# Weights converted without a clamp, their scale bounded by sums on TensorE, and a new table of homes for early work

## The chip, the cores and the metric

One core of one Trainium2 chip runs the whole program in one launch. The metric is the device time of one execution in microseconds (us); 514.47 us is the median of three runs of the kernel before (514.44 to 514.57).

Five engines work from instruction queues of their own: TensorE (PE; the loading of its stationary operand is listed apart as PEld), VectorE (DVE), ScalarE (ACT), GpSimd (POOL) and SyncE (SP, which here issues all DMAs).

## The reference

Windowed attention (8 batches, 8 heads, 576 positions, head size 64; a query sees itself and the 63 keys ahead of it), then a feed-forward block over all 4608 tokens (512 to 1024 to 512):

```python
scores = scale * np.matmul(q, k.transpose(0, 1, 3, 2))
scores = np.where((rel >= 0) & (rel < 64), scores, -1e9)
attn = softmax(scores); x = np.matmul(attn, v)        # tokens x 512
h = x @ w_in
solu = h * softmax(h)
ln = (solu - mean(solu)) / np.sqrt(var(solu) + 1e-6) * g_ln
return ln @ w_out
```

`w_in` and `w_out` come as 64-bit floats, all else as 32-bit ones.

## The kernel before

Tokens are worked through in 36 tiles of 128 (two windows of 64). For each tile: `scores` (TensorE, L547, into the bank pS), `softmax` (DVE, ACT; L599/L600 scale each head's row by its sum), the transposed probabilities PT (for tiles 0 to 7 `transposes` on TensorE, L654, and a copy, L659; later ones by two DMAs, L628 and L631), `values` (L680, bank pX), `moe_in` (bank pH, L707 for the first three tiles and L719 after), `moe_norm` (L734 largest value, L740 exponential, L743 product with h, which reads pH last, L751 squares, L758 power on POOL, L764 normalisation), `planes` and `turn` (halves of 16 bits, L792 and L795, and a transposing DMA) and `moe_out` (bank pO, L848 for the first tile and L858 after). pH, pS, pX and pO have one buffer each, so a tile's products there wait until the last reader of the tile before is through.

The weights are converted on the chip. `weight_block` does it for eight blocks of 1 MB (0 to 3 are w_in, 4 to 7 w_out). A block is loaded into raw (four buffers) as pairs of 32-bit words, low word first. ACT takes the absolute value of the high words, scaled by a power of two (L367, into w); POOL or DVE brings the top three bits of the low words to the bottom (L370 or L371); DVE clamps the result and keeps each partition's largest value (L374, `accum_out`), shifts it left by three and joins the low bits (L377), and sets the sign (L379). w then holds the weights as 32-bit floats with their exponent shifted.

The first tiles are multiplied with w directly, in 32 bits (`moe_in` for tiles 0 to 2, `moe_out` for tile 0). Later tiles use two 16-bit planes of each weight, high and low, made by `split`: L481/L482 (high) and L484 (low, always DVE). They need a common scale, which `spread` makes from the largest values of four blocks: a reduction (L390), two operations of one column (L392, L395), a diagonal matrix and a product with ones to spread the largest over all partitions (L398, L400), a reduction (L402) and two bit operations. `in_scale` does this for w_in while tile 1 is planned, `out_scale` for w_out in the turn of tile 3 behind `moe_out` of tile 0.

The order of instructions is a written-out list. Each operation is entered in `Plan` with engine, a duration in ns, and what it reads and writes. `order` computes when each is due, counted back from TensorE's own sequence, and then places them one by one, the most urgent that is ready first, with a latency of 150 ns between engines. Operations of TensorE that are marked loose may leave its sequence. Where TensorE would have nothing to do ahead of the first output (`shown`), `order` inserts fillers: 128x128 products of the identity into pO (L971), one for each 235 ns of 0.7 of the gap.

`HOMES` gives the engine for flexible operations, by task, tile and half; where it has no entry, a default holds (`home`): scale DVE for tiles 0 and 1 and else POOL; PT ACT, from tile 4 on DVE for the second half; join POOL up to tile 7 and then ACT; norm POOL; high planes ACT; planes POOL for tiles 1 and 2 and else DVE; high ACT; low bits POOL.

Of the kernel before, what the change touches and what calls it, by code (L numbers as in the profile page):

```python
# [11 lines left out]
BF16 = mybir.dt.bfloat16  # L12
# [20 lines left out]
W_SCALE = 2.0 ** 8  # L33
# [19 lines left out]
    ("scale", 0, 1): "POOL", ("scale", 1, 0): "POOL", ("scale", 1, 1): "ACT", ("scale", 3, 0): "DVE",  # L53
    ("scale", 4, 0): "ACT", ("scale", 4, 1): "DVE", ("scale", 5, 0): "ACT", ("scale", 5, 1): "ACT",
    ("scale", 6, 0): "ACT", ("scale", 6, 1): "ACT", ("scale", 8, 0): "DVE", ("scale", 8, 1): "DVE",
    ("scale", 10, 0): "ACT",
    ("PT", 0, 0): "DVE", ("PT", 1, 0): "DVE", ("PT", 1, 1): "DVE", ("PT", 2, 0): "DVE", ("PT", 4, 1): "ACT",
    ("PT", 5, 1): "ACT", ("PT", 6, 0): "DVE", ("PT", 7, 1): "ACT",
    ("join", 0, 0): "ACT", ("join", 1, 0): "ACT", ("join", 1, 1): "ACT", ("join", 3, 0): "ACT",
    ("join", 3, 1): "ACT", ("join", 4, 0): "ACT", ("join", 4, 1): "ACT",  # L60
    ("soft", 9, 0): "DVE", ("soft", 9, 1): "DVE", ("soft", 10, 0): "ACT", ("soft", 10, 1): "ACT",
    ("norm", 0, 1): "DVE", ("norm", 2, 0): "DVE", ("norm", 2, 1): "DVE", ("norm", 3, 1): "DVE",
    ("norm", 4, 0): "DVE", ("norm", 5, 1): "DVE",
    ("high planes", 2, 0): "DVE", ("high planes", 2, 1): "POOL", ("high planes", 3, 0): "POOL",
    ("high planes", 3, 1): "POOL", ("high planes", 4, 0): "POOL", ("high planes", 4, 1): "POOL",
    ("high planes", 5, 0): "POOL", ("high planes", 5, 1): "POOL", ("high planes", 6, 0): "DVE",
    ("high planes", 6, 1): "DVE",
    ("planes", 3, 0): "POOL", ("planes", 3, 1): "POOL", ("planes", 4, 0): "POOL", ("planes", 5, 0): "POOL", ("planes", 5, 1): "POOL", ("planes", 7, 0): "POOL",
    ("planes", 8, 0): "POOL",
    ("high", 1, 0): "DVE", ("high", 2, 0): "POOL", ("high", 2, 1): "POOL", ("high", 3, 0): "POOL",  # L70
    ("high", 4, 1): "POOL", ("high", 7, 0): "POOL",
    ("low bits", 4, 0): "DVE",
# [23 lines left out]
class Plan:  # L96
# [125 lines left out]
def tile_window_attention_solu_moe(  # L222
# [331 lines left out]
    def softmax(t):  # L554
# [10 lines left out]
        elif t in MASKED:  # L565
            for r in range(2):
# [4 lines left out]
                plan.op("DVE", 80, lambda hs=hs: nc.vector.tensor_scalar_mul(  # L571
# [71 lines left out]
    def transposes(t):  # L643
        if t >= SOFT_BY_DMA:
            return
        for x in range(2):
# [5 lines left out]
            def emit(x=x, pA=pA):  # L652
# [6 lines left out]
                e, 600, lambda x=x, pA=pA, e=e: copy_on(e)(PT(t)[:, 4 * x:4 * x + 4], pA()),  # L659
# [13 lines left out]
    def values(t):  # L673
# [16 lines left out]
        plan.op("ACT", 600, lambda: nc.scalar.mul(X(t, 0), PX(t), XS(t, 1)), [("pX", t), ("xs", t)], [("xH", t)])  # L690
        plan.op("DVE", 690, lambda: nc.vector.scalar_tensor_tensor(
# [32 lines left out]
    def moe_norm(t):  # L724
# [12 lines left out]
        if scaled:  # L737
            plan.op("DVE", 80, lambda: nc.vector.tensor_scalar(
# [7 lines left out]
        plan.op("DVE", 80, lambda: nc.vector.tensor_scalar_mul(nmean(), sp(), -1.0 / DFF), [key(2)], [key(4)])  # L746
        plan.op("DVE", 80, lambda: nc.vector.tensor_scalar(
# [38 lines left out]
    def planes(t):  # L786
        if not crosses(t):
            return
        for h in range(2):
# [5 lines left out]
            plan.op(e, {"POOL": 1450, "DVE": 690}[e], lambda hs=hs, e=e: units[e].tensor_sub(  # L795
# [41 lines left out]
    def moe_out(t):  # L837
# [24 lines left out]
        def ot():  # L862
# [158 lines left out]
```

## Time and profile before

| | us |
|---|---|
| median of three runs | 514.47 |
| profiled execution, its own time | 513.94 |
| its span | 512.0 |
| PE busy | 498.4 (97%) |
| DVE busy | 393.8 (77%) |
| ACT busy | 343.5 (67%) |
| POOL busy | 267.7 (52%) |
| fillers (L971), 166 of them, part of PE busy | 22.7 |

The profile is of one execution. The span runs from the first to the last instruction; the execution's own time lies 1.94 us above it. A busy time is the sum of an engine's instructions in a stretch without overlap. [...] A number in brackets behind an instruction is the idle time of its engine ahead of it, with what released it.

### The profile page before, as it was taken

Reading aid. Unit: us, or ns where it says so; the run is one execution under the profiler, and the core shown is the slowest. Engines: PE = TensorE matmul, PEld = TensorE weight load, DVE = VectorE, ACT = ScalarE, POOL = GpSimd, SP = SyncE. Lnnn points to the kernel's source line nnn. Section 1 sums busy time; section 2 is a strip of 40 time slices with the busy share of each in tenths; the row PEclk is TensorE's granted clock in tenths of the full one; section 3 lists DMA queues with packets and bytes.
Section 4 is the critical chain, followed back from the end, with each engine's and each line's share of the span. In section 5 each row is a group of like instructions: output and inputs, shape, how many; then the busy total and the mean of one; then the engine's idle time right before and its main releaser. Section 6 shows DMA issues by size and latency. Waiting matters only on the chain.

```text
span 512.0 us, 11781 instructions
## 1 busy us (share of the span) xinstructions
PE 498.4 (97%) x4297; PEld 269.3 (53%) x4297; DVE 393.8 (77%) x890; ACT 343.5 (67%) x978; POOL 267.7 (52%) x459
## 2 busy tenths in 40 slices
PE   8899989999999999999999999999999999999996
PEld 8575654455555555555555545555555555544452
DVE  4999999989778788888777777777777777765430
ACT  5378677787876677777777767777777777764240
POOL 5626515468555655555366656666666666662110
PEclk9999999999999999999999999999999999999999
DMA  8990316578999999999999999999999999769311
GB/s 348 402 359 33 90 56 156 173 190 199 283 247 268 247 268 255 258 292 259 263 258 253 262 250 249 255 270 268 267 276 227 262 272 229 186 176 235 104 41 42
DMA packets 157449, 115.59 MB, mean 226 GB/s; under 512 B 129872, under 2 KB 130128, under 8 KB 156880
## 3 DMA queue, kind: packets, MB, share of 16 engines
q1 hardware_dynamic: 157392, 114.84, 84.6%
q8 instruction: 34, 0.56, 0.4%
q14 instruction: 23, 0.19, 0.1%
HBM read 41.42 MB, written 41.42 MB: 162 GB/s over the span
## 4 chain that ended last, share of the span: by engine, by line
PE 81%; DVE 9%; DMA 3%; SPq 2%; ACT 1%; issue 1%; ACTq 0%
PE pO L858 31%; PE pH L719 30%; PE pX L680 7%; PE pS L547 6%; DMA raw<-pd 3%; PE pH L707 2%; SPq L804 1%; PE pO L848 1%; DVE w_inL L484 1%; DVE e L743 1%; PE t L654 1%; PE pX L858 1%; DVE w_outL L484 1%; DVE mst L734 1%; PE pO_filler L971 1%; DVE w L377 1%
## 5 line engine op out<-in xcount | busy, mean ns | idle before, releaser
L858 PE MATMUL pO<-w_outH,yT 128*128 128x512 f16 x544 | 167.6, 380 | 0.3 <-ACT ot L869 0.3
L719 PE MATMUL pH<-w_inH,xH 128*128 128x512 f16 x528 | 161.8, 379 | 2.4 <-DVE mst L743 2.1
L600 POOL TENSOR_SCALAR sS<-sS,rec 128x128 f32<-128x128 f32 x240 | 100.9, 439 | 101.6 <-DVE rec L596 101.0
L858 PEld LDWEIGHTS <-yT 128*128 128x128 f16 x840 | 79.6, 98 | 97.8 <-issue 6.2
L719 PEld LDWEIGHTS <-xH 128*128 128x128 f16 x792 | 75.1, 98 | 91.0 <-ACT xH L690 2.2
L584 ACT ACTIVATE sS<-sS,nmx 128x128 f32<-128x128 f32 x264 | 102.0, 390 | 18.1 <-DVE nmx L580 12.8
L858 PE MATMUL pO<-w_outL,yT 128*128 128x512 f16 x272 | 103.1, 379 | 0.7 <-DVE w_outL L484 0.7
L719 PE MATMUL pH<-w_inL,xH 128*128 128x512 f16 x264 | 99.0, 379 | 0.0
L758 POOL TENSOR_TENSOR mst<-mst,neghalf 128x1 f32<-128x1 f32 x36 | 20.3, 564 | 91.0 <-DVE mst L756 82.4
L740 ACT ACTIVATE e<-pH,mst,xscale 128x1024 f32<-128x1024 f32 x33 | 39.6, 1201 | 39.0 <-DVE rec L593 30.1
L734 DVE TENSOR_REDUCE mst<-pH 128x1 f32<-128x1024 f32 x36 | 44.0, 1223 | 26.6 <-PE pH L719 26.4
L869 ACT ACTIVATE ot<-pO,bound 128x512 f32<-128x512 f32 x34 | 23.3, 685 | 57.5 <-PE t_x L451 47.8
L764 POOL TENSOR_SCALAR e<-e,mst 128x512 f32<-128x512 f32 x66 | 52.0, 795 | 16.9 <-DVE mst L759 14.6
L620 POOL COPY raw<-sS 128x1024 uint16<-128x1024 uint16 x52 | 52.8, 1043 | 1.1 <-DVE sS L600 1.1
L795 DVE TENSOR_TENSOR pl<-e,pl 128x512 f16<-128x512 f32 x55 | 49.0, 926 | 1.7 <-ACT pl L792 1.6
L584 ACT ACTIVATION_READ_ACCUMULATOR sS<-sS,nmx 128x1 f32 x264 | 50.0, 189 | 0.0
L743 DVE CUSTOM_DVE_ANT_0 e<-pH,e 128x1024 f32<-128x1024 f32 x36 | 43.7, 1215 | 3.0 <-ACT e L740 3.0
L751 ACT ACTIVATE unread<-e,mst 128x1024 bf16<-128x1024 f32 x36 | 40.9, 1137 | 5.7 <-DVE mst L746 5.7
L754 DVE SCALAR_TENSOR_TENSOR mst<-mst 128x1 f32<-128x1 f32 x36 | 27.1, 752 | 21.8 <-ACT unread L751 21.8
L547 PE MATMUL pS<-qk 64*64 64x128 f32 x1152 | 39.8, 275 | 0.0
L575 DVE SCALAR_TENSOR_TENSOR sS<-pS,maskNone 128x1024 f32<-128x1024 f32 x26 | 31.7, 1221 | 9.9 <-PE pS L547 9.9
L514 ACT COPY vx<-v 64x512 f32<-64x512 f32 x63 | 38.9, 617 | 0.4
(129 smaller groups left out, 708.0 us busy)
## 6 DMA issues: line engine op xcount, KB each, us to landing
qk<-qk SPq DMA_DIRECT2D x36, 640.0 KB, 4.8
yd<-pl SPq DMA_DIRECT2D x33, 512.0 KB, 3.3
pd<-raw SPq DMA_DIRECT2D x28, 512.0 KB, 4.1
v<-vS SPq DMA_DIRECT2D x36, 256.0 KB, 3.6
y<-ot SPq DMA_DIRECT2D x35, 256.0 KB, 3.3
raw<-w_in SPq DMA_DIRECT2D x4, 1024.0 KB, 10.7
raw<-w_out SPq DMA_DIRECT2D x4, 1024.0 KB, 8.0
yT<-yd SPq DMA_TRANSPOSE x33, 5.1
```

Of the source, the lines that this page charges most:

```text
L547: nc.tensor.matmul(PS(t)[half * WIN:(half + 1) * WIN, r, p], q[rs, p, half * WIN:(half + 1) * WIN], keys, start=t not in MASKED, stop=t no ...
L584: plan.op("ACT", 580, lambda h=h: nc.scalar.activation(SS(t)[:, h], PS(t)[:, h // NPAIR, h % NPAIR] if t in MASKED else SS(t)[:, h], AF.Ex ...
L600: SS(t)[:, h], SS(t)[:, h], rec()[:, h:h + 1]) if e == "ACT" else units[e].tensor_scalar(
L620: plan.op(e, {"POOL": 1050, "ACT": 1000, "DVE": 700}[e], lambda x=x, e=e: copy_on(e)(PP(t)[:, :, 4 * x:4 * x + 4].rearrange("p k h n -> p ...
L719: plan.op("PE", 218, lambda n=n, c=c, k=k, w=w: nc.tensor.matmul(PH(t)[:, hs], X(t, k)[:, c], w(c, h), start=(n == 0), stop=(n == len(pass ...
L734: plan.op("DVE", 1230, lambda: nc.vector.tensor_reduce(nmax(), PH(t), axis=AX.X, op=ALU.max, negate=True), [("pH", t)], [key(0)])
L740: plan.op("ACT", 1320, lambda: nc.scalar.activation(E(t), PH(t), AF.Exp, bias=nmax(), scale=XS(t, 2) if scaled else 1.0, accum_out=se()), ...
L743: plan.op("DVE", 1310, lambda: nc.vector.tensor_tensor_reduce(E(t), PH(t), E(t), scale=1.0, scalar=0.0, op0=ALU.mult, op1=ALU.add, accum_o ...
L751: plan.op("ACT", 1330, lambda: nc.scalar.activation(unread, E(t), AF.Square, bias=nmean(), scale=1.0, accum_out=ss()), H2 + [key(4)], [key ...
L764: plan.op(e, {"POOL": 820, "DVE": 400}[e], lambda h=h, hs=hs, e=e: units[e].tensor_scalar(E(t)[:, hs], E(t)[:, hs], nmean(), kk(), ALU.add ...
L795: plan.op(e, {"POOL": 1450, "DVE": 690}[e], lambda hs=hs, e=e: units[e].tensor_sub(PL(t)[:, 1, hs], E(t)[:, hs], PL(t)[:, 0, hs]), [("e", ...
L858: plan.op("PE", 216, lambda f=f, i=i, x=x, k=k, y=y, w=w: nc.tensor.matmul(PO(), Y(t, y)[:, f], w(i, x), start=(f == k == 0), stop=(f == N ...
```

## The change

The clamp L374 goes. The first bit operation now reads w and writes its result into the low words of raw, the second joins the sign and writes w. The scale's bound is no longer the largest value but a sum: `add_up` takes the top 16 bits of each low word of raw (which then hold the absolute weight) as bf16, and multiplies 128 columns of them at a time, as the stationary operand, with one column of ones, eight products added up in one column of a PSUM tile `sums` in the bank pO. `spread` reduces four such columns. One small operation of `spread` goes. The powers of two of the scale are fitted to it. The fillers now write into `sums` too, and `shown` looks for the first tile's output alone.

```diff
-SHIFT = 2.0 ** -48
+SHIFT = 2.0 ** -112
-W_SCALE = 2.0 ** 8
+W_SCALE = 2.0 ** 13
...
-                shown = any(k[0] == "pO" for k in self.ops[i][4])
+                shown = ("pO", 0) in self.ops[i][4]
...
-        plan.op("DVE", 1210, lambda: nc.vector.tensor_scalar(
-            tf(), tf(), EXP_HI * SHIFT, EXP_LO * SHIFT, ALU.min, ALU.max, accum_out=most), [W],
-            [W, ("most", i)], lat=200)
-        plan.op("DVE", 1240, lambda: nc.vector.scalar_tensor_tensor(
-            t(), t(), 3, lo(), ALU.logical_shift_left, ALU.bitwise_or), [R, W], [W])
-        plan.op("DVE", 1240, lambda: nc.vector.scalar_tensor_tensor(
-            t(), hi(), -0x80000000, t(), ALU.bitwise_and, ALU.bitwise_or), [R, W], [W])
+        plan.op("DVE", 1270, lambda: nc.vector.scalar_tensor_tensor(
+            lo(), t(), 3, lo(), ALU.logical_shift_left, ALU.bitwise_or), [W], [R])
+        plan.op("DVE", 1380, lambda: nc.vector.scalar_tensor_tensor(
+            t(), hi(), -0x80000000, lo(), ALU.bitwise_and, ALU.bitwise_or), [R], [W])
+    def add_up(i):
+        def emit():
+            raw = T("raw", i, [P, 2, 512, 2], I32)
+            tops = raw.rearrange("p a n w -> p (a n w)").bitcast(BF16)
+            for c in range(8):
+                nc.tensor.matmul(
+                    sums()[:, P + i:P + i + 1], tops[:, 4 * c * P + 1:4 * (c + 1) * P:4], onesB[:, :1],
+                    start=(c == 0), stop=(c == 7))
+        plan.op("PE", 500, emit, [("raw", i), ("pO", "sums")], [("most", i)], loose=True)
+    def sums():
+        return T("pO", "sums", [P, DM], pool=ps_o)
...
     def spread(blocks, m, b, inv, name, gain=None):
+        for i in blocks:
+            add_up(i)
...
         small(lambda: nc.vector.tensor_reduce(
-            m, bound[:, blocks.start:blocks.stop], axis=AX.X, op=ALU.max), [("most", i) for i in blocks], [("m", name)])
-        small(lambda: nc.vector.tensor_scalar(
-            b.bitcast(I32), m.bitcast(I32), 3, 0, ALU.logical_shift_left, ALU.bitwise_or),
-            [("m", name)], [("b", name)])
+            m, sums()[:, P + blocks.start:P + blocks.stop], axis=AX.X, op=ALU.max),
+            [("most", i) for i in blocks] + [("pO", "sums")], [("m", name)], 150)
...
-                    T("pO", "filler", [P, DM], pool=ps_o)[:, :P], ident, ident, start=True, stop=True)
+                    sums()[:, :P], ident, ident, start=True, stop=True)
```

The durations in the list, in ns:

| operation | before | after |
|---|---|---|
| DVE passes of one column (`small` and others) | 80 | 145 |
| L367 on ACT; L370 on POOL | 1090; 1900 | 1150; 1330 |
| high on ACT, DVE, POOL; L484 | 600, 400, 860; 690 | 720, 490, 800; 840 |
| join on POOL, ACT, DVE | 700, 590, 400 | 880, 615, 400 |
| scale on POOL, DVE, ACT | 480, 220, 400 | 480, 340, 390 |
| PT on ACT, DVE | 600, 600 | 600, 680 |
| L690; L691; L869 | 600; 690; 580 | 680; 740; 680 |
| norm on POOL, DVE | 820, 400 | 820, 600 |
| planes on POOL, DVE | 1450, 690 | 1160, 920 |

The homes, defaults filled in, of both halves of tiles (for high and low bits: of blocks); what stays is left out, and so are tiles 7 to 12, for which the new table also has entries:

| task | before, then after |
|---|---|
| scale | 0: DVE POOL, ACT POOL; 1: POOL ACT, ACT POOL; 2: POOL POOL, ACT POOL; 3: DVE POOL, POOL POOL; 4: ACT DVE, POOL POOL; 5: ACT ACT, POOL ACT; 6: ACT ACT, POOL POOL |
| PT | 0: DVE ACT, ACT ACT; 1: DVE DVE, ACT DVE; 4: ACT ACT, DVE ACT; 6: DVE DVE, DVE ACT |
| join | 0: ACT POOL, POOL ACT; 1: ACT ACT, DVE DVE; 3: ACT ACT, DVE ACT; 4: ACT ACT, ACT POOL; 5: POOL POOL, ACT POOL |
| norm | 0: POOL DVE, POOL POOL; 2: DVE DVE, POOL POOL; 3: POOL DVE, POOL POOL; 4: DVE POOL, POOL DVE; 5: POOL DVE, POOL POOL; 6: POOL POOL, POOL DVE |
| high planes | 1: ACT ACT, ACT DVE; 2: DVE POOL, POOL POOL; 3: POOL POOL, DVE DVE; 5: POOL POOL, ACT DVE |
| planes | 3: POOL POOL, POOL DVE; 5: POOL POOL, DVE POOL; 6: DVE DVE, POOL POOL |
| high | 0: ACT ACT, POOL ACT; 1: DVE ACT, DVE POOL; 2: POOL POOL, ACT ACT; 3: POOL ACT, POOL ACT; 4: ACT POOL, DVE POOL; 5: ACT ACT, POOL POOL; 6: ACT ACT, POOL ACT |
| low bits | 1: POOL, DVE |

## Rows read from the trace of the kernel before

**Rows 1.** Busy time of each engine in three stretches (us, busy, instructions; then clock, DMA).

```profile
5.00:40.00 35.00, 32.11 (x350) 24.91 (x347) 31.58 (x65) 21.48 (x66) 13.26 (x21) 1.00 0.98 384
40.00:105.00 65.00, 60.95 (x508) 34.92 (x507) 64.10 (x153) 47.85 (x138) 30.07 (x38) 1.00 0.39 102
105.00:500.00 395.00, 393.94 (x3392) 202.77 (x3391) 297.65 (x673) 271.72 (x773) 220.20 (x380) 1.00 0.94 238
```

**Rows 2.** The same view of line L971 (fillers) alone: TensorE's products, weight loads.

```profile
5.00:40.00 35.00, 15.05 (x120) 14.06 (x120) 1.00 0.98 384
40.00:105.00 65.00, 4.30 (x32) 4.03 (x32) 1.00 0.39 102
```

**Rows 3.** Timeline of TensorE, 0 to 112 us: start, length, line, tile, count, wait.

```profile
24.96 3.96 PE L971 MATMUL pO_filler<-ident 128*128 128x128 f32 x34
...
39.33 7.11 PE L707 MATMUL pH<-w,xH 128*128 128x512 f32 x16 [0.35 <-DVE mst L743]
...
63.14 0.18 PE L451 MATMUL t_x<-vmost,some 128*128 128x2 bf16 x1
63.18 1.58 PE L971 MATMUL pO_filler<-ident 128*128 128x128 f32 x12
66.88 0.38 PE L719 MATMUL pH<-w_inH,xH 128*128 128x512 f16 x1 [2.12 <-DVE mst L743]
...
76.67 7.13 PE L848 MATMUL pO<-w,yF 128*128 128x512 f32 x16
```

**Rows 4.** Groups by line, 0 to 110 us: count, busy us, mean ns, idle before.

```profile
L379 DVE SCALAR_TENSOR_TENSOR w<-raw,w 128x1024 int32<-128x1024 int32 x8 | 11.0, 1376 | 0.0
...
L374 DVE TENSOR_SCALAR_CACHE_REDUCE w<-w 128x1024 f32<-128x1024 f32 x8 | 9.7, 1209 | 1.6 <-ACT w L367 1.6
...
L764 POOL TENSOR_SCALAR e<-e,mst 128x512 f32<-128x512 f32 x4 | 4.4, 1108 | 1.3 <-DVE mst L759 0.8 <-ACT sS L599 0.5
...
L600 DVE TENSOR_SCALAR sS<-sS,rec 128x128 f32<-128x128 f32 x12 | 3.6, 350 | 0.0
...
L764 DVE TENSOR_SCALAR e<-e,mst 128x512 f32<-128x512 f32 x4 | 2.5, 614 | 0.0
```

**Rows 5.** Busy time of line L374 alone, in two stretches.

```profile
5.00:40.00 35.00, 6.10 (x10) 1.00 0.98 384
40.00:105.00 65.00, 3.64 (x6) 1.00 0.39 102
```

**Rows 6.** Timeline of DVE, 0 to 106 us.

```profile
23.01 1.21 DVE L374 TENSOR_SCALAR_CACHE_REDUCE w<-w 128x1024 f32<-128x1024 f32 x1
...
24.15 1.21 DVE L379 SCALAR_TENSOR_TENSOR w<-raw,w 128x1024 int32<-128x1024 int32 x1
...
27.23 1.21 DVE L379 SCALAR_TENSOR_TENSOR w<-raw,w 128x1024 int32<-128x1024 int32 x1
...
44.01 0.14 DVE L746 TENSOR_SCALAR mst<-mst 128x1 f32<-128x1 f32 x1
44.07 0.14 DVE L748 TENSOR_SCALAR mst<-mst 128x1 f32<-128x1 f32 x1
...
72.73 1.21 DVE L377 SCALAR_TENSOR_TENSOR w<-w,raw 128x1024 int32<-128x1024 int32 x1
```

**Rows 7.** Timeline of ACT, 0 to 106 us.

```profile
18.51 1.17 ACT L367 ACTIVATE w<-raw 128x1024 f32<-128x1024 f32 x1 [0.93 <-DMA raw<-w_in]
...
102.60 2.44 ACT L599 ACTIVATE sS<-sS,rec 128x128 f32<-128x128 f32 x8
```

**Rows 8.** Timeline of POOL, 0 to 130 us.

```profile
20.06 1.96 POOL L370 TENSOR_SCALAR raw<-raw 128x1024 int32<-128x1024 uint32 x1
...
43.05 4.83 POOL L600 TENSOR_SCALAR sS<-sS,rec 128x128 f32<-128x128 f32 x8 [10.43 <-DVE rec L596]
...
109.80 2.80 POOL L600 TENSOR_SCALAR sS<-sS,rec 128x128 f32<-128x128 f32 x8 [0.67 <-DVE rec L596]
```

**Rows 9.** Line L451: instructions, count, shortest, median, longest in ns.

```profile
L451 PEld LDWEIGHTS <-some x33: 95/98/100, 52.6 to 467.8; 128*128 128x128 bf16 x33
```

More of the change, by code (lines that the diff above doesn't have):

```diff
@@ L52 @@
 HOMES = {
[L53 to L70, printed above, removed]
@@ L71 @@
-    ("high", 4, 1): "POOL", ("high", 7, 0): "POOL",
-    ("low bits", 4, 0): "DVE",
+    ("PT", 1, 1): "DVE", ("PT", 2, 0): "DVE", ("PT", 4, 0): "DVE", ("PT", 4, 1): "ACT", ("PT", 5, 1): "ACT",
+    ("PT", 6, 0): "DVE", ("PT", 6, 1): "ACT", ("PT", 7, 0): "DVE", ("high", 0, 0): "POOL", ("high", 1, 0): "DVE",
+    ("high", 1, 1): "POOL", ("high", 3, 0): "POOL", ("high", 4, 0): "DVE", ("high", 4, 1): "POOL",
+    ("high", 5, 0): "POOL", ("high", 5, 1): "POOL", ("high", 6, 0): "POOL", ("high", 7, 0): "POOL",
@@ new lines @@
+    ("high planes", 1, 1): "DVE", ("high planes", 2, 0): "POOL", ("high planes", 2, 1): "POOL",
+    ("high planes", 3, 0): "DVE", ("high planes", 3, 1): "DVE", ("high planes", 4, 0): "POOL",
+    ("high planes", 4, 1): "POOL", ("high planes", 5, 1): "DVE", ("high planes", 6, 0): "DVE",
+    ("high planes", 6, 1): "DVE", ("high planes", 7, 0): "POOL", ("high planes", 7, 1): "DVE",
+    ("high planes", 8, 0): "POOL", ("high planes", 8, 1): "DVE", ("high planes", 9, 1): "DVE",
+    ("high planes", 10, 0): "POOL", ("high planes", 10, 1): "POOL", ("high planes", 11, 0): "POOL",
@@ new lines @@
+    ("high planes", 11, 1): "POOL", ("join", 0, 1): "ACT", ("join", 1, 0): "DVE", ("join", 1, 1): "DVE",
+    ("join", 3, 0): "DVE", ("join", 3, 1): "ACT", ("join", 4, 0): "ACT", ("join", 5, 0): "ACT",
+    ("join", 7, 0): "ACT", ("join", 8, 0): "DVE", ("join", 10, 0): "DVE", ("join", 10, 1): "POOL",
+    ("join", 11, 1): "DVE", ("join", 12, 0): "DVE", ("join", 12, 1): "DVE", ("low bits", 1, 0): "DVE",
+    ("low bits", 4, 0): "DVE", ("norm", 4, 1): "DVE", ("norm", 6, 1): "DVE", ("norm", 7, 1): "DVE",
@@ new lines @@
+    ("norm", 8, 1): "DVE", ("norm", 9, 0): "DVE", ("norm", 10, 0): "DVE", ("norm", 10, 1): "DVE",
+    ("norm", 11, 0): "DVE", ("norm", 12, 0): "DVE", ("norm", 12, 1): "DVE", ("planes", 3, 0): "POOL",
+    ("planes", 4, 0): "POOL", ("planes", 5, 1): "POOL", ("planes", 6, 0): "POOL", ("planes", 6, 1): "POOL",
+    ("planes", 7, 1): "POOL", ("planes", 8, 0): "POOL", ("planes", 9, 0): "POOL", ("planes", 9, 1): "POOL",
+    ("planes", 10, 1): "POOL", ("planes", 11, 1): "POOL", ("planes", 12, 0): "POOL", ("planes", 12, 1): "POOL",
@@ L73 @@
+    ("scale", 0, 0): "ACT", ("scale", 0, 1): "POOL", ("scale", 1, 0): "ACT", ("scale", 1, 1): "POOL",
+    ("scale", 2, 0): "ACT", ("scale", 5, 1): "ACT", ("scale", 8, 1): "DVE", ("scale", 9, 1): "ACT",
+    ("scale", 11, 0): "ACT", ("scale", 11, 1): "ACT", ("scale", 12, 1): "DVE", ("soft", 8, 0): "DVE",
+    ("soft", 8, 1): "ACT", ("soft", 9, 1): "ACT", ("soft", 10, 0): "DVE", ("soft", 10, 1): "ACT",
+    ("soft", 11, 0): "DVE",
 }
@@ L315, in tile_window_attention_solu_moe @@
     bound = const.tile([P, NW + 12], F32, name="bound")
+    onesB = const.tile([P, 2], BF16, name="onesB")
+    nc.gpsimd.memset(onesB, 1.0)
     some = const.tile([P, P], BF16, name="some")
@@ L480, in split @@
             o = home("high", i, x, "ACT")
-            plan.op(o, {"ACT": 600, "DVE": 400, "POOL": 860}[o], lambda x=x, gain=gain, o=o: nc.scalar.mul(
+            plan.op(o, {"ACT": 720, "DVE": 490, "POOL": 800}[o], lambda x=x, gain=gain, o=o: nc.scalar.mul(
                 WH(i, x), W32(i)[:, x], gain()) if o == "ACT" else units[o].tensor_scalar(
                 WH(i, x), W32(i)[:, x], gain(), 0.0, ALU.mult, ALU.add), W + [G], [H])
-            plan.op("DVE", 690, lambda x=x, gain=gain: nc.vector.scalar_tensor_tensor(
+            plan.op("DVE", 840, lambda x=x, gain=gain: nc.vector.scalar_tensor_tensor(
                 WL(i, x), W32(i)[:, x], gain(), WH(i, x), ALU.mult, ALU.subtract),
@@ L513, in join @@
             e = home("join", t, x, "POOL" if t < JOINS else "ACT")
-            plan.op(e, {"POOL": 700, "ACT": 590, "DVE": 400}[e], lambda e=e, rows=rows, u=u: copy_on(e)(
+            plan.op(e, {"POOL": 880, "ACT": 615, "DVE": 400}[e], lambda e=e, rows=rows, u=u: copy_on(e)(
                 VX(t)[rows], V(u)[rows]), [("v", u)], [("vx", t, x)])
@@ L598, in softmax @@
             e = home("scale", t, h // NPAIR, "POOL" if t >= SCALES else "DVE")
-            plan.op(e, {"POOL": 480, "DVE": 220, "ACT": 400}[e], lambda h=h, e=e: nc.scalar.mul(
+            plan.op(e, {"POOL": 480, "DVE": 340, "ACT": 390}[e], lambda h=h, e=e: nc.scalar.mul(
                 SS(t)[:, h], SS(t)[:, h], rec()[:, h:h + 1]) if e == "ACT" else units[e].tensor_scalar(
@@ L658, in transposes @@
             plan.op(
-                e, 600, lambda x=x, pA=pA, e=e: copy_on(e)(PT(t)[:, 4 * x:4 * x + 4], pA()),
+                e, 600 if e == "ACT" else 680, lambda x=x, pA=pA, e=e: copy_on(e)(PT(t)[:, 4 * x:4 * x + 4], pA()),
                 [("t", n)], [("PT", t, x)])
@@ L689, in values @@
             return
-        plan.op("ACT", 600, lambda: nc.scalar.mul(X(t, 0), PX(t), XS(t, 1)), [("pX", t), ("xs", t)], [("xH", t)])
-        plan.op("DVE", 690, lambda: nc.vector.scalar_tensor_tensor(
+        plan.op("ACT", 680, lambda: nc.scalar.mul(X(t, 0), PX(t), XS(t, 1)), [("pX", t), ("xs", t)], [("xH", t)])
+        plan.op("DVE", 740, lambda: nc.vector.scalar_tensor_tensor(
             X(t, 1), PX(t), XS(t, 1), X(t, 0), ALU.mult, ALU.subtract),
@@ L763, in moe_norm @@
             e = home("norm", t, h, "POOL")
-            plan.op(e, {"POOL": 820, "DVE": 400}[e], lambda h=h, hs=hs, e=e: units[e].tensor_scalar(
+            plan.op(e, {"POOL": 820, "DVE": 600}[e], lambda h=h, hs=hs, e=e: units[e].tensor_scalar(
                 E(t)[:, hs], E(t)[:, hs], nmean(), kk(), ALU.add, ALU.mult),
@@ L794, in planes @@
             e = home("planes", t, h, "POOL" if t < PLANES else "DVE")
-            plan.op(e, {"POOL": 1450, "DVE": 690}[e], lambda hs=hs, e=e: units[e].tensor_sub(
+            plan.op(e, {"POOL": 1160, "DVE": 920}[e], lambda hs=hs, e=e: units[e].tensor_sub(
                 PL(t)[:, 1, hs], E(t)[:, hs], PL(t)[:, 0, hs]), [("e", t, h), ("pl", t, h)], [("pl", t, h, 1)])
```

23 lines of the change are left out of this document (10 added, 13 removed).

## The prediction

> **What bounds the kernel now.** I read the busy times of all engines by stretches first, then TensorE's stand-in matmuls (L971, whose product nobody reads), then the order of work on TensorE and on DVE. In the stretches the reader is to compare TensorE with its span: from 105 to 500 us it is busy 393.94 of 395 us, so what is left at 105 us simply runs off [rows 1]. All that can be gained lies ahead of 105. There TensorE's busy share deceives, since fillers count: from 5 to 40 us it sat idle for 35 - 32.11 = 2.9 us and ran 15.05 us of fillers, from 40 to 105 us idle for 4.05 and fillers for 4.30 [rows 1, 2]. Call both waste: 17.9 us in the first part and 8.4 in the second, 26.3 us in all. DVE is the engine with none: 31.58 of 35 us and 64.10 of 65 [rows 1].
>
> The order on TensorE says where the waste hangs on DVE. 34 fillers stand from 24.96 to about 28.9 us, while DVE ends the conversion of the fourth w_in block (L379 at 27.23, until 28.4) [rows 3, 6]. The next tile's products start at 39.33, released by DVE's L743, which frees the only pH buffer; those at 66.88 wait 2.12 us for the same, behind twelve fillers from 63.18 [rows 3]. But the first block cannot come sooner because of DVE: the first part is also full of loads (DMA share 0.98) [rows 1], and the fourth block's ACT pass begins at 18.51 [rows 7].
>
> **Removed: the clamp (L374), eight times.** It lasts 1209 ns [rows 4], but the next instruction starts 1.14 us behind it (23.01 to 24.15) [rows 6], so DVE gets back 8 x 1.14 = 9.1 us. Five of the eight lie ahead of 40 us (6.10 of the 9.74 us busy), three behind it [rows 5].
>
> **Changed: the two bit operations.** They stay two, but the first now writes the strided low words of raw. No row has that output. Nearest are DVE's passes with a strided input: 1.21 us undisturbed [rows 6], 1376 ns as a mean with two delayed ones [rows 4]. Per block that is nothing to 0.17 us more, 1.3 us for eight, and I see no reason for a gain over 0.07 us. I take 0.
>
> **Moved by the table of homes.** I count tiles 0 to 5, which are what precedes 105 us. DVE loses the scaling of twelve heads (tiles 0, 3, 4) at 350 ns, two PT copies against one that it gets, and four half-tile normalisations (tiles 0, 2, 2, 3) at 614 ns: 4.2 + 0.7 + 2.5 = 7.4 us [rows 4]; the 0.7 of the copy is an estimate, one 128x512 pass with PSUM as source, set a little over L764's. It gains three joins, two high planes net, one low plane, one half of a w_out block and one low-bits pass. Taken as eight half-tile passes of 614 ns that is 4.9 us [rows 4], and between 3 and 7 us if these passes are cheaper or dearer than L764. Net relief: 2.5 us, bounds 0.4 to 4.4; in spacing instead of durations nearer 1.5. I take 1.5, so that with the clamp DVE is relieved of 10.6 us before 105 us.
>
> **The scheduler's durations.** They alter no instruction, only the order. Small DVE passes go from 80 to 145 in the list, which is their duration, while two of them start 0.06 us apart (44.01 and 44.07) [rows 6]. So the new list believes DVE fuller than it is. Behind 105 us this has room: DVE is busy 297.65 of 395 us and ACT 271.72 [rows 1]. I cost it at nothing there, and up to 1 us (as much as TensorE is idle there now) if a tile's order turns out badly.
>
> **Added: 64 products of one column (add_up).** Each needs its own weights. The nearest row is L451, bf16 weights of 128x128 and two columns: load 95 to 100 ns [rows 9], product 0.18 us, and the filler behind it starts 0.04 us later [rows 3]. Bounds: 64 x 0.04 = 2.6 us, and 64 x (0.10 + 0.18) = 17.9 us if nothing overlapped. [...] For w_in (32 of them) they stand where fillers stand, in 17.9 us of waste, and cost nothing; without that cover, 3.2 us. For w_out they fall into the second part and take 3.2 of its 8.4 us.
>
> **Added: a wait.** The first tile's output (L848 at 76.67) may not begin until the sums of all eight blocks are read, since they share the one pO bank. Behind it on TensorE stand the next tile's products and everything else; ahead of the read on DVE may stand two or three passes of 1.14 us. Today's last L377 starts at 72.73 and ends at 73.9 [rows 6]; 0.15 us for signals (the list's figure), 0.8 us of sums, the same signal and a short reduction lead to 75.1, 1.5 us ahead of 76.67 [rows 3]. I cost it at 0, upper bound 3.4 us. The slot of raw is also held until its sum is made; what waits for it are the loads of w_out, whose blocks DVE takes up last.
>
> **Sum.** First part: with the clamp gone DVE could end block four 4 x 1.14 + 0.8 (scaling of tile 0) = 5.4 us sooner. But its data set a floor: low bits start on POOL at 20.06 and take 1.96 [rows 8], then two DVE passes, 22.0 + 2.3 = 24.3 against 28.4, so 4.1 us. Fillers already placed and the scores between them will eat some; but a pass less ahead of L743 at 39.33 gives some back. I take 4.0, bounds 2 to 5.8. Second part: relief is 10.6 - 5.4 = 5.2 us, from a waste of 8.4 of which the sums take 3.2; these two meet at 5.2, and never will every wait close. I take half, 2.5, bounds 0 to 5.2. Together 6.5 us. The profiled execution had a span of 512.0 and a time of 513.94 us, the runs a median of 514.47; 505.5 of span gives 507.4 there and **508.0** as a median.
>
> **A rule against the change.** POOL's eight scalings took 4.83 us from 43.05 and 2.80 from 109.80 [rows 8]: the same work is 1.7 times dearer in the crowded part, where DVE runs its splits of weights. [...]
>
> **Rivals.**
> First, *the relief passes through whole*: every us that DVE gets back comes out, as both parts are DVE's. For it: 64.10 of 65 us. Against: loads and the fourth block's arrival. The 1.3 us that the fourth block's arrival denies are not lost, for DVE has other work to put there, which is then out of the second part's way: 10.6 us, 503.9.
> Second, *POOL takes DVE's place* (the slower side). Scaling of tiles 3, 4 and 6 goes wholly to POOL. At the crowded price that is 4.83 us a tile against 2.44 on ACT for eight heads [rows 7, 8], 2.4 us later for each of three tiles' transposes; normalisations of tiles 0, 2 and 3 go to POOL at 1108 against 614 ns [rows 4], half of which are serial: some 1 us a tile. In all 7.2 + 3 = 10.2 us of waiting on TensorE: 3.7 more than is saved, 518.2. It decides once over 6.5 of these 10.2 us reach TensorE. For it: the 4.83 us. Against: POOL is busy 30.07 of 65 us in that part [rows 1], and scores run tiles ahead.
> Third, *nothing comes of it*: the list puts more fillers in, the sums and the wait for pO take 3.2 + 3.4 us more than counted, which is all of the 6.5. 514.4. For it: DMA share 0.98. Against: block four waited 4 us for DVE alone.
>
> **How the numbers follow.** The forecast has a chance of 0.50 (505.0 to 511.5), the first rival 0.23, the second 0.15, the third 0.12. The range from 501.5 to 515.0 leaves out most of the second rival and the far end of the first. Below 0.2% (1.0 us) a measurement here cannot tell a change from none. Faster takes the forecast and the first rival whole, 0.73; the third gives 0.11 to no change and the rest, with the second, to slower: 0.16.
>
> **What would show it.** L374 is gone and DVE's work ahead of the fourth tile's output falls by about 10 us; fillers fall from 19 to some 12 us busy; the first tile's last L707 products start 3 to 4 us sooner, and so do those of the second and third tile; eight sums of a block take 0.3 to 0.8 us; from there to the end the distance stays within 1 us of today's. It is wrong if TensorE waits for POOL's L600, L764 or L795 before 105 us, if L848 waits for a reduction, or if the sums take over 1.5 us a block.

## The result and the profile after

The changed kernel takes 508.29 us as a median of four runs (505.68 to 510.18), the kernel before 514.46 (513.50 to 514.57). The ratio is 0.9874 with a 95% interval of 0.9832 to 0.9917, so 6.2 us are gained; 508.0 was forecast. Here and below medians, ranges and ratios are of undisturbed runs alone, and a ratio need not be the quotient of the medians. The profiled execution took 508.81 us, with a span of 506.6 (512.0 before).

Busy times by stretches in the changed kernel, to be read beside [rows 1] (PE, PEld, DVE, ACT, POOL, then TensorE's granted clock as a share of full speed, DMA share, GB/s):

```profile
5.00:40.00 35.00, 33.19 (x343) 23.39 (x344) 28.95 (x64) 25.27 (x81) 16.39 (x22) 1.00 0.94 386
40.00:105.00 65.00, 61.85 (x607) 36.69 (x606) 61.79 (x134) 47.43 (x143) 45.39 (x65) 1.00 0.43 121
105.00:500.00 395.00, 391.15 (x3324) 200.55 (x3322) 300.52 (x680) 260.39 (x735) 211.60 (x369) 1.00 0.90 235
```

And the fillers alone, now L989, beside [rows 2] (products, weight loads):

```profile
5.00:40.00 35.00, 9.61 (x70) 8.53 (x70) 1.00 0.94 386
40.00:105.00 65.00, 2.50 (x18) 2.18 (x18) 1.00 0.43 121
```

Idle time ahead of 105 us fell from 6.9 to 1.8 + 3.2 = 5.0 us, fillers from 19.4 to 12.1, as forecast. DVE's busy time ahead of the fourth tile's output fell from 111.3 us (to 123.54) to 99.8 (to 115.56); a fall of about 10 was forecast. Behind 105 us the sign turns: TensorE is idle for 3.85 of 395 us, where it was 1.06.

TensorE's timeline gives the places to compare with [rows 3] (L725 is L707 of before, L866 L848, L737 L719, L876 L858, L390 the sums):

```profile
26.29 3.70 PE L725 MATMUL pH<-w,xH 128*128 128x512 f32 x8
...
34.68 7.10 PE L725 MATMUL pH<-w,xH 128*128 128x512 f32 x16
...
59.89 0.38 PE L737 MATMUL pH<-w_inH,xH 128*128 128x512 f16 x1
...
69.49 0.70 PE L390 MATMUL pO_sums<-onesB,raw 128*128 128x1 bf16 x16
71.29 7.10 PE L866 MATMUL pO<-w,yF 128*128 128x512 f32 x16 [1.11 <-DVE mst L772]
...
96.56 0.38 PE L737 MATMUL pH<-w_inH,xH 128*128 128x512 f16 x1
...
102.08 0.39 PE L876 MATMUL pO<-w_outH,yT 128*128 128x512 f16 x1 [0.65 <-DMA yT<-yd]
...
107.30 0.38 PE L737 MATMUL pH<-w_inH,xH 128*128 128x512 f16 x1
```

Two more rows of the kernel before answer to 26.29 and 96.56:

```profile
29.89 3.70 PE L707 MATMUL pH<-w,xH 128*128 128x512 f32 x8
...
105.25 0.38 PE L719 MATMUL pH<-w_inH,xH 128*128 128x512 f16 x1
```

A 32-bit product stands as two records in these views: the first output's 16 are eight products, and the 34 and twelve fillers of the prediction are 17 and six. Their lengths are not touched by that. The first tile's last products start 3.6 us sooner, the second tile's 4.65 (34.68 against 39.33), the fourth's 7.0 (59.89 against 66.88), the first output 5.4 (71.29 against 76.67, after a wait of 1.11). The second half of the sixth tile's products is 8.7 us ahead, and at 102.08 stands the first wait for a DMA. From 8.7 the lead falls to the 5.4 us of the spans. In the line of 71.29 the wait is put down to L772, a small pass of another tile; what the products need is the reduction of the sums (L410), which DVE ended just ahead of it. Who made TensorE wait in the changed kernel (total us, times, longest):

```profile
PE pO L876 <- DMA yT<-yd: 2.5, 3, 1.0
PE t L672 <- POOL sS L618: 1.8, 2, 1.0
PE pX L698 <- DMA raw<-pd: 1.8, 3, 1.1
...
PE pO L866 <- DVE mst L772: 1.1, 1, 1.1
```

4.3 us of these are for the DMAs that transpose (yT, and raw for the probabilities); the kernel before has 0.8 of them, all behind 105 us.

### The profile page after: what moved, and what is told of

Its sections match the earlier page's. It is cut to its first block, busy times and chain, and to the rows that moved or that the text cites. A ratio compares the mean times of both kernels' runs of the same rounds, so it can differ in the third digit from the quotient of the medians.

```text
span 506.6 us, 11800 instructions
## 1 busy us (share of the span) xinstructions
PE 492.7 (97%) x4297; PEld 265.0 (52%) x4297; DVE 391.7 (77%) x875; ACT 334.8 (66%) x958; POOL 277.5 (55%) x477
## 4 chain that ended last, share of the span: by engine, by line
PE 70%; DMA 9%; DVE 5%; SPq 4%; POOL 3%; ACT 1%; issue 1%; ACTq 0%
PE pO L876 29%; PE pH L737 26%; PE pX L698 6%; PE pS L565 5%; DMA raw<-pd 4%; DMA yT<-yd 3%; SPq L822 2%; PE pH L725 1%; SPq L649 1%; PE pX L876 1%; DMA yd<-pl 1%; POOL w_outH L500 1%; DVE raw L378 1%; DVE mst L752 1%; DVE e L761 1%
## 5 line engine op out<-in xcount | busy, mean ns | idle before, releaser
L876 PE MATMUL pO<-w_outH,yT 128*128 128x512 f16 x544 | 167.7, 380 | 2.7 <-DMA yT<-yd 2.5
L737 PE MATMUL pH<-w_inH,xH 128*128 128x512 f16 x528 | 161.8, 379 | 0.3 <-DVE xH L709 0.3
L618 POOL TENSOR_SCALAR sS<-sS,rec 128x128 f32<-128x128 f32 x252 | 102.4, 425 | 79.3 <-DVE rec L614 60.8
L876 PEld LDWEIGHTS <-yT 128*128 128x128 f16 x840 | 79.6, 98 | 99.6 <-issue 4.7
L737 PEld LDWEIGHTS <-xH 128*128 128x128 f16 x792 | 75.1, 98 | 89.2 <-DVE xH L709 0.8
L876 PE MATMUL pO<-w_outL,yT 128*128 128x512 f16 x272 | 103.1, 379 | 0.0
L737 PE MATMUL pH<-w_inL,xH 128*128 128x512 f16 x264 | 99.0, 379 | 0.0
L782 POOL TENSOR_SCALAR e<-e,mst 128x512 f32<-128x512 f32 x62 | 50.8, 826 | 50.3 <-DVE mst L756 31.6
L708 ACT ACTIVATE xH<-pX,xscale 128x512 f16<-128x512 f32 x33 | 22.7, 687 | 43.9 <-PE pX L698 43.6
L638 POOL COPY raw<-sS 128x1024 uint16<-128x1024 uint16 x50 | 50.7, 1040 | 0.2
L813 DVE TENSOR_TENSOR pl<-e,pl 128x512 f16<-128x512 f32 x49 | 39.5, 809 | 2.0 <-ACT pl L810 1.9
L598 DVE TENSOR_REDUCE nmx<-sS 128x8 f32<-128x1024 f32 x32 | 38.5, 1202 | 0.0
## 6 DMA issues: line engine op xcount, KB each, us to landing
yd<-pl SPq DMA_DIRECT2D x33, 512.0 KB, 3.4
pd<-raw SPq DMA_DIRECT2D x28, 512.0 KB, 4.0
```

What stands on the lines that cost most here:

```text
L618: SS(t)[:, h], SS(t)[:, h], rec()[:, h:h + 1]) if e == "ACT" else units[e].tensor_scalar(
L638: plan.op(e, {"POOL": 1050, "ACT": 1000, "DVE": 700}[e], lambda x=x, e=e: copy_on(e)(PP(t)[:, :, 4 * x:4 * x + 4].rearrange("p k h n -> p ...
L737: plan.op("PE", 218, lambda n=n, c=c, k=k, w=w: nc.tensor.matmul(PH(t)[:, hs], X(t, k)[:, c], w(c, h), start=(n == 0), stop=(n == len(pass ...
L782: plan.op(e, {"POOL": 820, "DVE": 600}[e], lambda h=h, hs=hs, e=e: units[e].tensor_scalar(E(t)[:, hs], E(t)[:, hs], nmean(), kk(), ALU.add ...
L813: plan.op(e, {"POOL": 1160, "DVE": 920}[e], lambda hs=hs, e=e: units[e].tensor_sub(PL(t)[:, 1, hs], E(t)[:, hs], PL(t)[:, 0, hs]), [("e", ...
L876: plan.op("PE", 216, lambda f=f, i=i, x=x, k=k, y=y, w=w: nc.tensor.matmul(PO(), Y(t, y)[:, f], w(i, x), start=(f == k == 0), stop=(f == N ...
```

## The experiments

Theory A is the prediction's: DVE's relief ahead of 105 us sets the gain; after the result it has a second half, that part of it is given back behind 105 us in waits for transposing DMAs. Rival C gives the gain to the new list and homes. Beside each median stand the lowest and highest run.

**The changed kernel again**, twice, without an edit.

> The changed kernel as it is, beside the kernel before, to see how far its runs lie apart (505.7 to 510.2 us in four, against 513.5 to 514.6 before). Theory A (the extra spread is waiting for transposing DMAs behind 105 us, which TensorE now reaches 8 us sooner): runs between 505 and 511, and the profile shows 2 to 4 us of TensorE waits for DMAs, where the kernel before has 0.8. Rival B (the spread comes from the early part): waits for DMAs stay near those of the first profile while the early marks move by microseconds.

> The changed kernel once more, as the measure for the other three on the same chip: 507.5 to 509.5 us as a median, six runs within 5 us of one another.

509.22 us (506.88 to 509.97; ratio 0.9891, 0.9868 to 0.9914) and 508.92 (505.91 to 511.74; 0.9876, 0.9845 to 0.9908). The kernel before, run 23 and 17 times beside them, lay between 512.91 and 517.01, so the close runs that the first expectation started from were luck. Some extra spread is left, 6.1 us in the changed kernel's sixteen runs against 4.1 (the six of the third set lie 5.8 us apart, not within 5). Waits for DMAs of 3.7 and 2.3 us are in the range that A gave, but B has a part too: the sixth tile's second half starts at 96.56, 97.86 and 95.72 us in the three profiles. The clock does not make the gain: in the runs with a mean granted clock of 0.999 or 1.000 alone, the changed kernel takes 505.68 to 509.09 us and the one before 512.91 to 516.01. The profile with 2.3 has the shortest span of the three, 503.7:

```profile
PE pO L876 <- DMA yT<-yd: 1.5, 4, 0.7
PE pX L698 <- DMA raw<-pd: 0.8, 2, 0.4
```

The other shows something that nobody had expected. Stretches of 2.5 us around the first output:

```profile
67.50:70.00 2.50, 2.25 (x69) 1.93 (x64) 2.50 (x4) 1.88 (x6) 1.22 (x2) 1.00 0.22 48
70.00:72.50 2.50, 1.61 (x3) 0.71 (x4) 2.50 (x15) 1.07 (x1) 0.72 (x2) 0.74 0.86 302
72.50:75.00 2.50, 2.50 (x5) 1.13 (x4) 2.50 (x4) 2.48 (x8) 2.50 (x4) 0.58 0.04 16
75.00:77.50 2.50, 2.50 (x7) 1.07 (x6) 2.50 (x7) 1.09 (x2) 2.50 (x5) 1.00 0.00 0
```

The granted clock (third number from the end) falls to 0.74 and 0.58, right behind a wait of 1.14 us at 69.75; the products of the first output take 8.80 us instead of 7.10:

```profile
70.89 8.80 PE L866 MATMUL pO<-w,yF 128*128 128x512 f32 x16 [1.14 <-DVE mst L772]
```

**The clamps put back** on DVE, list and homes untouched.

```diff
+        def both():
+            nc.vector.tensor_scalar(tf(), tf(), BIG, 0.0, ALU.min, ALU.max,
+                accum_out=bound[:, i:i + 1])
+            nc.vector.scalar_tensor_tensor(lo(), t(), 3, lo(), ...)
-        plan.op("DVE", 1270, lambda: nc.vector.scalar_tensor_tensor(lo(), t(), 3, lo(), ...
+        plan.op("DVE", 1270, both, [W], [R])
```

> The changed kernel, its list and its homes untouched, with the eight clamp passes put back on DVE just ahead of the first bit operation (values unchanged, nobody reads their sums). Theory A (DVE's relief is the cause): DVE carries 9.1 us more ahead of 105 us and at least 5 of them come out, 513 to 517 us. Rival C (the new list and homes are the cause, the clamp hung in DVE's idle time): within 1.5 us of the changed kernel, 507 to 510.

515.0 us (513.99 to 517.41), ratio 1.0018 (1.0002 to 1.0034): the whole gain is gone. A holds and C falls, but with two reservations. First, TensorE now waits 4.6 us in three waits ahead of the sums and 3.79 us for the first output, where the changed kernel has 0.6 and 1.1:

```profile
PE pO_sums L395 <- DVE raw L381: 4.6, 3, 1.9
...
73.86 0.69 PE L395 MATMUL pO_sums<-onesB,raw 128*128 128x1 bf16 x16
...
78.35 8.67 PE L871 MATMUL pO<-w,yF 128*128 128x512 f32 x16 [3.79 <-DVE mst L777]
```

So the new bank rule makes the clamp dearer than it was: DVE's delay reaches TensorE through the sums. Second, TensorE's granted clock falls behind three of these waits (1.94, 1.82 and 3.79 us), to 0.51, 0.50 and 0.62 in the stretches of 2.5 us that stand here:

```profile
20.00:22.50 2.50, 2.50 (x37) 2.16 (x36) 2.41 (x4) 0.00 (x0) 0.00 (x0) 0.51 1.03 417
...
47.50:50.00 2.50, 2.50 (x32) 2.26 (x33) 2.50 (x4) 1.59 (x4) 0.00 (x0) 0.50 0.00 0
...
77.50:80.00 2.50, 1.65 (x2) 0.83 (x3) 2.50 (x15) 1.11 (x2) 0.76 (x2) 0.62 0.03 14
```

Its rows give an estimate of the price: the values' products take 1.98 us instead of 1.15 at 20.55 and at 48.65, the first output 8.67 instead of 7.10, together some 3 us. All twelve runs have a mean granted clock of 0.983 to 0.993, against 0.992 to 1.000 in the changed kernel's sixteen. By this estimate about half of what the clamps cost here is the clock behind the waits and not DVE's time itself.

**The clamps of the w_in blocks alone** put back (the same edit under `if i < NC`).

> The changed kernel, its list untouched, with the clamp put back for the four w_in blocks alone. Theory A with the prediction's split of the gain (4.0 us before 40 us, from the w_in blocks, 2.5 us after): 3 to 5 us slower than the changed kernel. Rival H (the w_out blocks carry the gain, since the first part is held by the loads): under 2 us slower.

510.06 us (507.50 to 512.91; ratio 0.9895, 0.9866 to 0.9924) against 508.92 beside it: 1.1 us by the medians, and the intervals overlap. H's number fits and the 3 to 5 us of the prediction's split do not, though the intervals would still allow some 3 us. In its profile the second tile's products start at 36.32, 1.6 us later than in the changed kernel. H's reason, the loads, is not what shows: DVE has room there now and waits for POOL's low bits, 5.0 us in all. First and second bit operation in the changed kernel, up to 110 us (count, busy, mean ns, idle before):

```profile
L378 DVE SCALAR_TENSOR_TENSOR raw<-w,raw 128x1024 int32<-128x1024 int32 x8 | 10.1, 1275 | 5.1 <-POOL raw L375 5.0
...
L381 DVE SCALAR_TENSOR_TENSOR w<-raw 128x1024 int32<-128x1024 int32 x8 | 9.8, 1227 | 0.0
```

**The conversion alone**, with the old homes and durations.

```diff
-HOMES = { ... new ... }
+HOMES = { ... old ... }
-def small(emit, reads, writes, cost=145):
+def small(emit, reads, writes, cost=80):
... (and each other duration in the list that the conversion does not add)
```

> The new conversion and the sums alone, with the old homes and the old durations of all that stays. Theory A: most of the gain, 507 to 510 us. Rival C: under 2 us of gain, 512.5 to 515.

**The list alone**: the kernel before with the new homes and durations, the same edit the other way.

> The kernel before with the new homes and the new durations, its clamp kept. Theory A: little, 512 to 516 us, since DVE stays as full as it was ahead of 105 us. Rival C: most of the gain, 507 to 510.

509.68 us (509.42 to 511.58; ratio 0.9915, 0.9891 to 0.9940) and 513.70 (511.32 to 516.08; 0.9981, 0.9963 to 0.9998). The conversion gives some 4.4 us, the list some 1.0, both 5.6 to 6.5. By the totals these are A's numbers, not C's. TensorE's timelines say more (us from the start, one profile each):

| start of | before | changed | conversion alone | list alone | clamps back |
|---|---|---|---|---|---|
| second tile's products | 39.33 | 34.68 | 34.71 | 35.96 | 36.87 |
| fourth tile's products | 66.88 | 59.89 | 60.89 | 59.61 | 64.27 |
| first output | 76.67 | 71.29 | 74.61 | 68.74 | 78.35 |
| sixth tile's second half | 105.25 | 96.56 | 100.96 | 102.72 | 105.19 |
| span | 512.0 | 506.6 | 508.1 | 511.0 | 512.9 |

At the fourth tile's products and the first output the list alone, clamps kept, is earlier than the changed kernel. It loses its lead later, most of it at one place, where the second rival of the prediction can be seen at work: TensorE waits 3.18 us for POOL's scalings, for which DVE had the reciprocals ready late (the profile names L759, just behind them). Behind that wait the granted clock falls to 0.52:

```profile
100.03 2.90 PE L659 MATMUL t<-ident,sS 128*128 128x128 f32 x8 [3.18 <-POOL sS L605]
...
100.00:102.50 2.50, 2.47 (x8) 1.30 (x9) 1.86 (x3) 1.80 (x10) 2.50 (x8) 0.52 0.92 235
```

POOL in the same stretch:

```profile
91.96 2.27 POOL L800 TENSOR_TENSOR pl<-e,pl 128x512 f16<-128x512 f32 x2
99.61 2.79 POOL L605 TENSOR_SCALAR sS<-sS,rec 128x128 f32<-128x128 f32 x8 [5.37 <-DVE mst L759]
```

So the list alone does win time early; a DVE that the clamps keep full gives it away later.

**The sums made twice.**

```diff
-            for c in range(8):
+            for c in (*range(8), *range(8)):
```

> The changed kernel with every block's eight sums made twice over, the list unchanged. Theory A (a sum of a block takes 0.35 us on TensorE as profiled; only those directly ahead of the first output lie on the path): 0.7 us more, 509 to 510.5 us. Rival D (the sums are a real load of TensorE, as the prediction put them with 0.8 us a block): 2.5 us more or above, over 511.

507.21 us (504.95 to 509.21; ratio 0.9850, 0.9822 to 0.9879): not slower than the changed kernel (measured on other chips), so even the 0.7 us of A does not show. D falls. In its profile the sums ahead of the first output take 1.23 us, and the wait behind them shrinks to 0.64: most of the added time goes into that wait. In the changed kernel the load lasts longer than L451's (118 against 98 ns as medians [rows 9]), but sixteen pairs take 0.70 us together (at 69.49 in the timeline above), since the loads overlap: sixteen times 118 ns would be 1.9 us. Loads and products:

```profile
L390 PEld LDWEIGHTS <-raw x64: 111/118/132, 12.0 to 70.0; 128*128 128x128 bf16 x64
L390 PE MATMUL pO_sums<-onesB,raw x64: 167/172/194, 12.1 to 70.0; 128*128 128x1 bf16 x64
```

**The w_out sums reduced sooner**, measured twice.

```diff
-            [("most", i) for i in blocks] + [("pO", "sums")], [("m", name)], 150)
+            [("most", i) for i in blocks] + [("pO", "sums")], [("m", name)], 150,
+            1000 if name == "out" else 0)   # latency in the list
```

> The changed kernel with the reduction of w_out's sums due 1 us sooner in the list: the last two blocks' sums then stand ahead of the scores instead of behind them, and the reduction ahead of the last sign operation. Theory E (the 1.1 us wait ahead of the first tile's output, during which TensorE has nothing, is on the path, and its clock falls there in some executions): 1 us less without the clock's part and 1.5 to 2.5 less with it, 506 to 508, no stretch at half clock there, runs closer together. Rival B2 (that wait is made up later): 508 to 509.5.

> The version with the reduction of w_out's sums due 1 us sooner, beside the changed kernel on the same chip. Theory E: 1 to 2.5 us faster than it. Rival B2: within 0.7 us of it, since waits for DMAs behind 105 us take back what the early part wins.

506.67 us (505.41 to 510.81; ratio 0.9861, 0.9826 to 0.9896) and, beside the changed kernel's 508.92, 508.41 (505.72 to 512.63; 0.9844, 0.9813 to 0.9876). The wait at L866 is gone in both profiles, and in the first the output starts at 70.4 instead of 71.3. But no gain can be told from none: by the medians it is 0.5 us, by the ratios 1.6, and the intervals overlap. E and B2 are both left open, and the runs do not lie closer together, as E had it. The second profile (512.63 us) has 5.8 us of waits for DMAs from 90 us on:

```profile
PE pO L876 <- DMA yT<-yd: 3.2, 2, 2.1
PE pX L698 <- DMA raw<-pd: 2.6, 3, 2.1
```

**Fillers in the gap** ahead of the first output.

```diff
+            if i == NW - 1:
+                filler(10)()
```

> The changed kernel with ten fillers (1.2 us) behind the last block's sums, where TensorE waits for the reduction. Theory E's part on the clock: the wait is not shorter, but the clock does not fall, so the slowest runs go, 507 to 509 us. Rival F (the clock falls for another reason, or the fillers delay the first output): as slow as the changed kernel or up to 1 us slower, and half clock still shows at the first output.

507.74 us (507.13 to 511.60; ratio 0.9877, 0.9845 to 0.9909). The ten fillers (20 records) took 2.48 us, twice the 1.2 that was meant, and since they write into the tile of the sums, the reduction waited 1.44 us for them:

```profile
70.75 2.48 PE L991 MATMUL pO_sums<-ident 128*128 128x128 f32 x20
```

The first output starts at 73.57, 2.3 us later than in the changed kernel's profile (0.7 of it from the clock earlier on), and the time, on another chip, is none the longer. So the fillers do delay the first output, as F had it, and a delay there can be made up later, as B2 has it. In the profile the clock holds at the first output, but is 0.61 from 17.5 to 20 us and 0.71 from 20 to 22.5, where nothing was edited. Whether the fillers protect the clock is left open: one profile, and a place where it falls only in some executions.

**Less DMA traffic**, in the changed kernel and in the one before.

```diff
+            if 4 <= t < 32:
+                continue
             plan.dma(P * DM * 4 // len(parts), lambda cs=cs: nc.sync.dma_start(out[...
```

> The changed kernel without the stores of the output of tiles 4 to 31 (that part of the output is left out), 7 of some 116 MB of DMA traffic. Theory A's second half (2 to 3 us of the early gain are given back in waits for transposing DMAs): waits for DMAs fall below 1.5 us, 505 to 507. Rival G (the transposes are slow by themselves, or for their place in the queue): within 0.7 us of the changed kernel.

> The kernel before without the stores of the output of tiles 4 to 31 (that part is left out), the control to the same cut in the changed kernel, which gave 506.15 us against some 508.5. Theory A's second half (the changed kernel gives back part of its gain in waits for transposing DMAs, and the lighter traffic returns it): here the cut is worth under 1 us, 513.5 to 515, so that without these stores the change is worth 8 us. Rival G2 (lighter traffic helps either kernel alike): 2 us, 512 to 513.

506.15 us (505.71 to 506.98; ratio 0.9836, 0.9813 to 0.9858) for the changed kernel, 515.22 (513.44 to 515.76; 0.9989, 0.9975 to 1.0003) for the one before. By the medians the same cut is worth 2.1 to 3.1 us to the former and 0.3 to 0.6 to the latter; without these stores the change is worth 7.9 us by the ratios, 9.1 by the medians, instead of some 6.3. G2 falls. Waits for DMAs behind 105 us are 1.1 us in the changed kernel:

```profile
PE pO L876 <- DMA yT<-yd: 1.1, 1, 1.1
```

and from 90 us on 0.2 in the one before:

```profile
PE pX L680 <- DMA raw<-pd: 0.2, 1, 0.2
```

This speaks for A's second half and does not settle it. The two cuts were measured on different chips, and on the chip of the first the changed kernel itself was not run: its three variants there, with all their stores, lie only 0.5 to 1.6 us above 506.15, and two of their profiles (sums made twice, fillers in the gap) also have no more than 1.1 us of waits for DMAs. What the cut takes away is the slow end: five runs within 1.3 us, where each of the variants spreads over 4 us or more and the fastest of them (504.95) is faster still. It also takes 28 issues off SP's queue, so that traffic and queue are not told apart.

## Why the prediction was right, and where two errors met

**The bound.** Right: the gain was to be had ahead of 105 us and on DVE. Taking the clamp away from the old list gave most of it, putting it back in the new one took all, by the estimate above about half of that through the clock. The count of DVE's relief says tiles 0 to 5 and leaves out tile 5, where DVE loses one normalisation and gets two planes; that is some 0.6 us less relief and changes little.

**First part, forecast 4.0 us:** 4.65 at the second tile's products. The size is right and the working only half. A floor set by the low bits was real, only later than the 24.3 us reckoned: L378 of the fourth block starts at 23.62, after 1.71 us of waiting for POOL, and its partner ends at 26.6, 1.8 us sooner than the 28.4 of before and not 4.1. But the clamp is not the only way there. The list alone, clamps kept, brings the second tile's products to 36.0, and in the new list the w_in clamps cost only 1.1 us. At this mark the conversion alone gives as much as both together: DVE's relief by the homes and by the clamp fill the same gap, and there they do not add up. In the total they do (4.4 and 1.0 us, both 5.6 to 6.5).

**Second part, forecast 2.5 us:** 8.7 - 4.65 = 4.0 us at 96.56. The sums were mis-sized, 0.35 us a block instead of 0.8: 32 of them took 1.4 instead of 3.2 us of the waste. No run shows the 0.1 us a pair that stands behind the 0.8: the lower bound of 0.04 us was the right one, for in the changed kernel sixteen loads of 112 to 132 ns fill 0.61 us. That the second part gave more for this reason is argued, not shown. The timelines show another place, which the count up to tile 5 could not have: between the halves of the sixth tile's products stand the transposes of the next tile (number 6), and in the kernel before they waited for ACT's scalings and kept pace with them. In the changed kernel POOL had these scalings done in time:

```profile
103.04 2.38 PE L654 MATMUL t<-ident,sS 128*128 128x128 f32 x8 [0.91 <-ACT sS L599]
```

```profile
95.69 1.04 PE L672 MATMUL t<-ident,sS 128*128 128x128 f32 x8
```

0.91 + 2.38 - 1.04 = 2.25 us of the 4.0 arise here. The new homes and DVE's relief both have a part in it: with the old homes the transposes still take 2.02 us (conversion alone), with the new homes and a full DVE they wait 3.18 (list alone).

**The wait for pO, forecast 0:** 1.11 us, within its bound of 3.4. The prediction had named such a wait as a sign of being wrong; here it is too short to overturn the sum. The sums were not done 1.5 us ahead, as reckoned; those of the last two blocks stood behind the scores on TensorE, and their reduction (L410) behind the last sign operation (L381) on DVE, as its timeline shows:

```profile
23.62 1.23 DVE L378 SCALAR_TENSOR_TENSOR raw<-w,raw 128x1024 int32<-128x1024 int32 x1 [1.71 <-POOL raw L375]
...
69.87 1.20 DVE L381 SCALAR_TENSOR_TENSOR w<-raw 128x1024 int32<-128x1024 int32 x1
71.00 0.15 DVE L410 TENSOR_REDUCE bound<-pO_sums 128x1 f32<-128x4 f32 x1
71.07 0.20 DVE L772 SCALAR_TENSOR_TENSOR mst<-mst 128x1 f32<-128x1 f32 x1
```

**Behind 105 us, forecast within 1 us:** the step that failed. 2.8 us more of idle time stand there than before, and some 3.6 us of the waits there are for DMAs. DVE's and ACT's room was checked, that of the DMAs was not, though their share there was 0.94 in [rows 1]. A TensorE that arrives 8 us sooner finds transposes that have not landed. They are not slower as a rule: from issue to landing they take 5.1 (yT) and 5.9 us (raw) as medians, 5.1 and 6.0 before. Single ones are issued too late for it: the one that TensorE waits for at 129.22 was issued at 124.48, behind another that held SP's queue from 118.38 for 5.38 us. Whether the DMAs' load or the order in that queue is to blame stays open. The size of the loss is not fixed either: from the sixth tile's second half to the end the lead falls by 3.3, 2.6 and 1.2 us in the three profiles of the changed kernel. In the first of them the loss is about what the second part gained over the forecast, and so the total came out within 0.3 us of it; that is luck.

**What stood against the change.** POOL's scalings did go both ways again, 5.02 us for eight at 49.23, where DVE makes low planes (L502) for 3.92 us of them, and 2.80 at 57.28, where it makes none:

```profile
49.23 5.02 POOL L618 TENSOR_SCALAR sS<-sS,rec 128x128 f32<-128x128 f32 x8
...
57.28 2.80 POOL L618 TENSOR_SCALAR sS<-sS,rec 128x128 f32<-128x128 f32 x8 [2.50 <-DVE mst L777]
```

But the 4.83 us of the kernel before [rows 8] came with only 0.75 us of that line (there L484). Which of DVE's instructions make the difference, if any, is not shown. TensorE did wait for POOL's scalings ahead of 105 us, the prediction's other sign of being wrong, but only 1.8 us, at 16.7 and 18.0 us where fillers stood anyway; the second rival needed 6.5. With the old conversion, where DVE stays full, 3.2 us did reach it.

## What to carry to other kernels

When a change makes an early stage shorter, read the next stage's shared resource as if the work arrived that much sooner: here waits for DMA transposes took back between an eighth and some four tenths of the lead, by the profile. A pass that leaves the busiest engine is worth what nothing else can fill. Two remedies can fill the same early gap and still both be needed, so read a lead at several marks: one of them alone reached the first output earliest and lost its lead at the next stage. A scratch value put into a bank that the main product needs is a new edge in the order, and TensorE waited longer for it (1.11 us) than the sums ahead of it took (0.70). A wait may cost twice, by itself and by the clock behind it: behind one of 1.14 us the granted clock fell to 0.58 and the first output took 8.80 us, behind one of 1.11 us it held at 1.00 and the output took 7.10.

## What was not expected of the hardware

TensorE's granted clock fell for a short stretch in some executions and not in others of one program: in three profiles of the changed kernel once (to 0.74 and 0.58 at 70 to 75 us, behind a wait of 1.14 us). Ten of the fourteen profiles have a stretch of 2.5 us at 0.50 to 0.62 somewhere ahead of 500 us; where it hits the first output, the products take 8.67 to 8.80 us instead of 7.10. A product of one column with its own 128x128 bf16 weights, read at a stride of 8 bytes, has loads of 111 to 132 ns (95 to 100 packed) and yet a pitch of some 0.04 us (sixteen loads in 0.61). And the first bit operation with its strided output took 1275 ns as a mean, as much as its predecessor (1268).
